# Scale of the first tiles by one-element instructions, and low weights last in the first products

## The chip, the cores and the metric

The kernel runs on one core of one Trainium2 chip. The metric is the device time of one execution in microseconds (us). Five engines work side by side, each with an instruction queue of its own: PE (matrix products; PEld is its loading of weights), DVE (vector), ACT (scalar and activation), POOL (GpSimd) and SP, which here issues all DMAs. They wait for each other through semaphores.

## The reference

```python
x = A_x                                   # 1 x 2048 x 640
xn = _layernorm(x)                        # (x - mean) / sqrt(var + 1e-5)
s = _A_ref(xn, A_wqkv, A_wo)              # attention, 32 heads of 20, window of 8 keys at stride 2, then @ wo
g = _silu(_B_ref(xn, B_w_gate, B_w_up, B_w_down))   # ((xn @ w_gate) * (xn @ w_up)) @ w_down, 1536 wide
return x + s * g
```

Everything is float32.

## The kernel before

**Precision by split.** A matrix in float32 is kept as two matrices: a high part (`hi`, an ACT copy into the rounded type that PE reads, line 85 for weights and 213 for x) and a low part (`lo`, raw minus high, line 86 on POOL for the first weights, line 214 on DVE for x). A product is then three products that add up in one PSUM tile: high by high, then first high by second low, then first low by second high. `mm3` (lines 88 to 93) writes that order out: all K chunks of the first kind, all of the second, all of the third. For `qkv` the first operand is x and the second the weights; for `gate_up_half` the first is the weights and the second x.

**Tiles.** The 2048 positions are 16 tiles of 128 rows. K is 640, that is 5 chunks of 128. `norm(s, n)` normalises n tiles from tile s: `moments` (bn_stats and bn_aggr on DVE), `rstd` (lines 187 to 195), `apply` (line 198, one tensor_scalar of 128x640 per tile with mean and scale as per-row pointers). `trans(s)` (lines 210 to 214) transposes a tile on PE in two groups (4 chunks and 1), into PSUM tiles with tag `q`, of which there are 4; ACT writes the high part, DVE the low part. `rstd` takes a square root on ACT, a sum and a reciprocal on DVE, and corrects the reciprocal by one Newton step: 1.5 - 0.5 * (var + eps) * a * a, times a. It is called for tile 0, tile 1, tiles 2 and 3 together, tiles 4 to 7, and once for the 8 odd tiles.

**Order.** The schedule is manual: each engine executes in the order in which the program issues to it. The head of the program, from its line 616 on, is in turn: `norm(0, 1)`, `moments` of tile 1, the split of the first three chunks of the first attention weights, `trans(0)`, one idle product to keep PE at work, the split of the last two chunks, `norm(1, 1)`, `moments` of tiles 2 and 3, `qkv(0, 0)`, `trans(1)`, the split of the first gate and up weights in five pieces, `norm(2, 2)`, `qkv(0, 1)`, the split of the next gate and up weights, `gate_up_first`, `trans(2)`, `trans(3)`, then `norm(4, 4)` and the following tiles. `split_wq` and `split_wf` put the high parts on ACT and the low parts on POOL. Four idle products run ahead of all this (line 155).

`gate_up_first` (lines 408 to 413) does the first 256 columns, two tiles, of the gate and the up product of the first 128 features, since only two tiles are there by then; `gate_up(0, 0, part=part0)` does the other 256 later and evicts both.

**After the head.** 12 attention units (6 groups of heads by even and odd positions) run on DVE while PE computes the next `qkv` and gate and up pieces; then the output projection, the preparation of the down weights (`sum_wd`, `split_wd`), and the down product by a scheme of 7 products for 8 blocks (`product`), which ends the kernel.

Of the kernel before, what the change touches and what calls it, by code (L numbers as in the profile page):

```python
# [14 lines left out]
ALU = mybir.AluOpType  # L15
# [11 lines left out]
KD, KF = D // P, F // P  # L27
CH = 512
# [11 lines left out]
EPS = 1e-5  # L40
# [10 lines left out]
def kernel(  # L51
# [11 lines left out]
    nc = tc.nc  # L63
# [11 lines left out]
    def st(shape, tag, bufs, dt=F32):  # L75
        cnt[0] += 1
        return sb.tile(shape, dt, tag=tag, bufs=bufs, name=f"{tag}_{cnt[0]}")

    def pt(shape, tag, bufs):
        cnt[0] += 1  # L80
        return ps.tile(shape, F32, tag=tag, bufs=bufs, name=f"{tag}_{cnt[0]}")
# [3 lines left out]
        nc.scalar.activation(hi, raw, AF.Copy)  # L85
        eng.tensor_sub(lo, raw, hi.bitcast(F32))  # L86

    def mm3(acc, pairs, first=True, last=True):

        pairs = list(pairs)  # L90
        runs = [(a[i], b[j]) for i, j in ((0, 0), (0, 1), (1, 0)) for a, b in pairs]
        for n, (a, b) in enumerate(runs):
            nc.tensor.matmul(acc, a, b, start=first and n == 0, stop=last and n == len(runs) - 1)  # L93

# [20 lines left out]
    wf_raw, wf = {}, {}  # L115
# [51 lines left out]
    xT = []  # L167
# [10 lines left out]
    def moments(s0, n, mv=None):  # L178
        stats = st([P, n, 2, 6], "stats", 2)
        mv = st([P, n, 2], "mv", 2) if mv is None else mv  # L180
        for i in range(n):
            for a in range(2):
                nc.vector.bn_stats(stats[:, i, a, :], xt[s0 + i][:, a * HALF:(a + 1) * HALF])
            nc.vector.bn_aggr(mv[:, i, :], stats[:, i])
        return mv

    def rstd(var, out, n):
        r = st([P, 4, NE], "rstd", 2)[:, :, :n]
        nc.scalar.activation(r[:, 0, :], var, AF.Sqrt, bias=eps_t)
        nc.vector.tensor_scalar_add(r[:, 1, :], var, EPS)  # L190
        nc.vector.reciprocal(r[:, 2, :], r[:, 0, :])
        nc.vector.tensor_mul(r[:, 3, :], r[:, 2, :], r[:, 2, :])
        nc.vector.tensor_mul(r[:, 3, :], r[:, 3, :], r[:, 1, :])
        nc.vector.tensor_scalar(r[:, 3, :], r[:, 3, :], -0.5, 1.5, op0=ALU.mult, op1=ALU.add)
        nc.vector.tensor_mul(out, r[:, 3, :], r[:, 2, :])
# [4 lines left out]
    def norm(s0, n, mv=None):  # L200
        mv = moments(s0, n) if mv is None else mv
        r = st([P, n], "r", 2)
        rstd(mv[:, :, 1], r, n)
        for i in range(n):
            apply(xt[s0 + i], mv[:, i, 0:1], r[:, i:i + 1])

    def trans(s):
        hi, lo = xT_tile(s)
        for k0, k1 in ((0, 4), (4, KD)):
            p = pt([P, k1 - k0, P], "q", 4)  # L210
            for k in range(k0, k1):
                nc.tensor.transpose(p[:, k - k0, :], xt[s][:, k * P:(k + 1) * P], ident)
            nc.scalar.activation(hi[:, k0:k1, :], p, AF.Copy)  # L213
            nc.vector.tensor_sub(lo[:, k0:k1, :], p, hi[:, k0:k1, :].bitcast(F32))
# [52 lines left out]
            nc.gpsimd.memset(kv_t[u][0:1, :, 0:W - 1, :], 0.0)  # L267
            kv_zero[r] = GROUPS[g]

    def qkv(u, i):  # L270
        g, r = UN[u]
        c = GROUPS[g] * DH
        p = pt([P, 3 * c], "q", 4)
        hi, lo = xT[(r * NE + i) // TPC]
        t0 = (i % TPC) * P
        a, b = (hi[:, :, t0:t0 + P], lo[:, :, t0:t0 + P]), wq[g]
        mm3(p, [([t[:, k, :] for t in a], [t[:, k, :] for t in b]) for k in range(KD)])
        nc.scalar.activation(kv_t[u][:, :, W - 1 + i, :], p[:, c:].rearrange("p (a c) -> p a c", a=2), AF.Copy)  # L278
        nc.scalar.activation(q_t[u][:, i, :], p[:, :c], AF.Copy)
        for i0, i1 in ((1, 5), (5, NE)):  # L280
            if i == i1 - 1:
                for p0, p1 in ((0, 112), (112, 127)):
                    nc.sync.dma_start(kv_t[u][p0 + 1:p1 + 1, :, i0 - 1:i1 - 1, :],
                                      kv_t[u][p0:p1, :, W - 1 + i0:W - 1 + i1, :])
# [77 lines left out]
    credit = [0]  # L362


    def gate_up_half(f, ch, n, p, c=slice(0, CH)):
        mm3(p[:, c], [([t[:, k, n, :] for t in wf[f]], [t[:, k, c] for t in xT[ch]]) for k in range(KD)])

    def gate_up(f, ch, between=(), amid=(), part=None):
        if part is None:
# [2 lines left out]
        else:  # L372
            pp, c = part, slice(CH // 2, CH)
        gate_up_half(f, ch, 0, pp[0], c)
        for act in amid:
            act()
# [5 lines left out]
        finish_piece()  # L382
        advance(PACE * 3.25 * share)
        gate_up_half(f, ch, 1, pp[1], c)

        def finish():
# [21 lines left out]
    def gate_up_first(f, ch):  # L408

        pp = [pt([P, CH], "g", 2), pt([P, CH], "u", 2)]  # L410
        for n in range(2):
            gate_up_half(f, ch, n, pp[n], slice(0, CH // 2))
        return pp


# [2 lines left out]
    def load_wo(ks):  # L418
        t = st([P, 2, D], "wraw", 3)
        for n, k in enumerate(ks):  # L420
            nc.sync.dma_start(t[:, n, :], wo[:, k, :])
            wo_raw[k] = t[:, n, :]
        return t
# [33 lines left out]
    def out_proj(s):  # L457
        a = oT.pop(s)
        y = st([P, D], "gs", 2)
        for n in range(2):  # L460
            c = slice(n * HALF, (n + 1) * HALF)
            p = pt([P, HALF], "q", 4)
            mm3(p, [([t[:, k, :] for t in a], [t[:, c] for t in wo_s[k]]) for k in range(KD)])
            nc.scalar.activation(y[:, c], p, AF.Copy)
        nc.sync.dma_start(s_scr[s], y)
# [157 lines left out]
    norm(1, 1, mv1)  # L623
    begin_unit(0, False)
    mv2 = moments(2, 2)
    qkv(0, 0)
    trans(1)
    load_x(13, 1, xa[:, 1:2])
    split_wf(0, nc.gpsimd, range(KD + 1))
    norm(2, 2, mv2)  # L630
    qkv(0, 1)
    split_wf(1, nc.gpsimd, range(KD + 1))
    zero_front(0)
    part0 = gate_up_first(0, 0)
    trans(2)
    trans(3)
    mask = st([1, NE, W], "mask", 1)
    nc.gpsimd.memset(mask, 0.0)
    for i in range(NE - 1):
# [3 lines left out]
                          ident.rearrange("p (q i) -> p q i", i=QB).unsqueeze(2).to_broadcast([P, NQ, NQ, QB]))  # L643
    norm(4, 4)
    qkv(0, 2)
    qkv(0, 3)
    gate_up(0, 0, part=part0)
# [13 lines left out]
    load_xq(15, 1, xd)  # L661
    nc.vector.tensor_copy(mro[:, 0, :], mvo[:, :, 0])
    rstd(mvo[:, :, 1], mro[:, 1, :], NE)
    gate_up(0, 1, amid=(spread,))
    trans_odd(8)
# [61 lines left out]
    for ch in range(NCH):  # L727
        gate_up(f0, ch)
        if ch == 0:
# [3 lines left out]
            t = load_wo((4,))  # L733
# [20 lines left out]
    for s in range(NT):  # L754
        k, part = divmod(s - 1, 2)
# [27 lines left out]
    for m in range(n_prod):  # L783
        n, j = divmod(m, 7)
# [59 lines left out]
```

## Time and profile before

| | |
|---|---|
| median of 3 runs | 790.14 us (789.95 to 790.39) |
| the profiled execution | 791.53 us |
| its span | 789.7 us |
| granted PE clock, mean | 0.998 |
| PE busy | 779.9 us, 99% |
| DVE busy | 662.2 us, 84% |
| ACT, POOL busy | 235.0 us, 148.2 us |
| PE busy in 0 to 5, 5 to 10, 10 to 15, 15 to 20, 20 to 25 us | 3.63, 4.47, 4.05, 4.78, 4.54 us |

A row of the timeline gives the start and the duration in us, the engine, the line of the program, the operation, the tiles written and read with their shapes, and a count where equal rows were merged; in brackets stands how long the engine was idle before it and what ended that. The time of a DVE row runs from its issue to its end, so a row that is held by something shows a long duration, not an idle gap. Rows of one engine can overlap at their ends. A list of waits gives the engine and line that waited, the engine and tile it waited for, the sum in us, how often, and the longest.

### The profile page before, as it was taken

The page shows a single profiled execution, that of the slowest core. Times are in us where ns is not written, and L with a number is a line of the kernel's source. Part 1 is how long each engine was busy: PE and PEld are TensorE (multiplying, and loading weights), DVE is VectorE, ACT ScalarE, POOL GpSimd, SP SyncE. Part 2 cuts the span into 40 slices and gives each one's busy share as a digit, 9 for nine tenths or more (in the row PEclk, how much of TensorE's full clock was granted, in tenths as well). Part 3 has the DMA queues.
Part 4 walks back from the last instruction along what each step waited for, and adds up shares of the span by engine and source line. Part 5 has one row for each costly group of instructions (what it writes and reads, how often), then busy time and mean ns, then how long its engine had stood idle before and what let it go on. Part 6 is the DMA issues. An engine that isn't in the chain of part 4 may idle for free. (4 is left out here: it accounts for less than half of the span.)

```text
span 789.7 us, 11220 instructions
## 1 busy us (share of the span) xinstructions
PE 779.9 (99%) x4456; PEld 709.0 (90%) x4456; DVE 662.2 (84%) x657; ACT 235.0 (30%) x536; POOL 148.2 (19%) x110
## 2 busy tenths in 40 slices
PE   8999999999999999999999999999999999999997
PEld 6889898889898898898898989888889999999997
DVE  7889899999999979996999999991268667787775
ACT  4334211121112111311221212112256554444442
POOL 5201211022013200510231000113367600000000
PEclk9999999999999999999999999999999999999999
DMA  8272122141132322404033132322896574555533
GB/s 306 80 229 74 42 59 73 48 123 48 49 84 87 95 71 61 118 27 111 28 104 85 57 85 71 106 88 66 176 249 207 168 279 134 202 207 180 180 101 134
DMA packets 81517, 92.68 MB, mean 117 GB/s; under 512 B 23016, under 2 KB 63032, under 8 KB 81336
## 3 DMA queue, kind: packets, MB, share of 16 engines
q1 hardware_dynamic: 81464, 91.96, 38.1%
q8 instruction: 35, 0.57, 0.3%
q14 instruction: 18, 0.15, 0.1%
HBM read 54.53 MB, written 28.31 MB: 105 GB/s over the span
## 5 line engine op out<-in xcount | busy, mean ns | idle before, releaser
L93 PE MATMUL g<-xc,wf 128*128 128x512 f32 (+1 forms) x735 | 176.2, 390 | 0.1
L93 PE MATMUL u<-xc,wf 128*128 128x512 f32 (+1 forms) x735 | 176.1, 390 | 0.0
L93 PEld LDWEIGHTS u<-xc,wf 128*128 128x128 f32 x735 | 135.6, 187 | 32.2
L93 PEld LDWEIGHTS g<-xc,wf 128*128 128x128 f32 x735 | 135.3, 187 | 31.3 <-POOL wf L86 0.3
L93 PE MATMUL q<-wqh,xc 128*128 128x300 f32 (+1 forms) x960 | 159.9, 309 | 1.3 <-ACT xc L213 0.8
L93 PEld LDWEIGHTS q<-wqh,xc 128*128 128x128 f32 x960 | 146.1, 188 | 3.9 <-ACT xc L213 1.7
L310 DVE TENSOR_TENSOR t<-q,kv 128x1600 f32<-128x1600 f32 (+1 forms) x48 | 98.0, 2042 | 10.1 <-DMA kv<-kv 10.1
L331 DVE TENSOR_TENSOR t<-e,kv 128x1600 f32<-128x1600 f32 (+1 forms) x48 | 97.6, 2051 | 1.1
L86 POOL TENSOR_TENSOR wf<-wraw,wf 128x256 fp32r<-128x256 f32 (+2 forms) x22 | 49.8, 2281 | 247.5 <-ACT wf L85 247.5
L313 DVE TENSOR_REDUCE lg<-t 128x80 f32<-128x1600 f32 (+1 forms) x48 | 92.6, 1930 | 1.2
L378 ACT ACTIVATE gs<-g 128x512 f32<-128x512 f32 x48 | 28.7, 598 | 205.8 <-PE g L93 197.1
L93 PE MATMUL q<-wql,xc 128*128 128x300 f32 (+1 forms) x480 | 86.5, 310 | 0.5 <-POOL wql L86 0.4
L339 DVE TENSOR_TENSOR t<-t,t 128x1600 f32<-128x1600 f32 (+1 forms) x36 | 80.2, 2228 | 1.1
L93 PEld LDWEIGHTS q<-wql,xc 128*128 128x128 f32 x480 | 74.4, 188 | 0.9 <-POOL wql L86 0.9
L278 ACT ACTIVATE kv<-q 128x200 f32<-128x200 f32 (+1 forms) x96 | 33.5, 349 | 131.8 <-PE q L93 131.8
L586 PE MATMUL q<-xc,wf 128*128 128x320 f32 x432 | 67.3, 309 | 0.0
L586 PEld LDWEIGHTS q<-xc,wf 128*128 128x128 f32 x432 | 64.3, 188 | 0.0
L86 POOL TENSOR_TENSOR wql<-wraw,wqh 128x300 fp32r<-128x300 f32 (+4 forms) x15 | 34.0, 2297 | 141.7 <-ACT wqh L85 141.7
L93 PE MATMUL q<-wf,wf 128*128 128x320 f32 x156 | 36.2, 313 | 1.3 <-ACT wf L85 1.3
L93 PEld LDWEIGHTS q<-wf,wf 128*128 128x128 f32 x156 | 25.9, 188 | 2.2 <-ACT wf L85 2.0
L389 DVE TENSOR_TENSOR hs<-u,gs 128x512 f32<-128x512 f32 x39 | 26.6, 683 | 0.4 <-issue 0.4
L86 DVE TENSOR_TENSOR wf<-ot,wf 128x640 fp32r<-128x640 f32 x13 | 14.3, 1098 | 13.8 <-ACT wf L85 12.9
(157 smaller groups left out, 892.5 us busy)
## 6 DMA issues: line engine op xcount, KB each, us to landing
h_scr<-hs SPq DMA_DIRECT2D x48, 256.0 KB, 2.3
wraw<-in_wgu SPq DMA_DIRECT2D x12, 640.0 KB, 5.1
t<-h_scr SPq DMA_DIRECT2D x8, 768.0 KB, 7.6
s_scr<-gs SPq DMA_DIRECT2D x16, 320.0 KB, 3.5
hs<-s_scr SPq DMA_DIRECT2D x16, 320.0 KB, 4.4
gs<-in_x SPq DMA_DIRECT2D x16, 320.0 KB, 4.9
out<-q SPq DMA_DIRECT2D x15, 320.0 KB, 2.4
wraw<-h_scr SPq DMA_DIRECT2D x12, 384.0 KB, 5.6
```

Source lines behind the costliest of these rows:

```text
L86: eng.tensor_sub(lo, raw, hi.bitcast(F32))
L93: nc.tensor.matmul(acc, a, b, start=first and n == 0, stop=last and n == len(runs) - 1)
L278: nc.scalar.activation(kv_t[u][:, :, W - 1 + i, :], p[:, c:].rearrange("p (a c) -> p a c", a=2), AF.Copy)
L310: nc.vector.tensor_mul(t, q.rearrange("p i c -> p (i c)").unsqueeze(1).to_broadcast([P, 2, NE * c]), places(0, j))
L313: nc.vector.tensor_reduce(out=lg[:, :, j:j + 2].rearrange("p n a -> p a n"), in_=heads(t), op=ALU.add, axis=AX.X)
L331: nc.vector.tensor_mul(heads(t), pw, heads(places(1, j)))
L339: nc.vector.tensor_add(acc, acc, t)
L378: nc.scalar.activation(gs, pp[0], AF.Copy)
L389: nc.vector.tensor_mul(hs, pp[1], gs)
L586: nc.tensor.matmul(p, y[:, i, k], wd_t[name][k][:, l], start=new and r == 0, stop=r == len(runs) - 1, skip_group_check=True)
```

## The change

Three edits.

In `rstd`, where one or two tiles are normalised, the instructions work on one element per partition. The sum with eps is one instruction per tile. After the reciprocal, the two multiplications, the Newton factor and the last multiplication (four instructions, three of them tensor_tensor with two tensors as inputs) become three tensor_scalar instructions per tile, with the other factors as per-row pointers: b = a * a * ve, then b = -0.5 * b + 1.5, then out = b * a. For one tile that is 5 DVE instructions in place of 6, for two tiles 9 in place of 6. Calls with four or eight tiles keep the old form.

In the first call of `qkv` the order of the three kinds of products becomes high by high, low part of x by high weights, high part of x by low weights.

In `gate_up_first` the products with low weights of both the gate and the up part come after all others; the partial sums stay open in their two PSUM tiles in between.

The number of products does not change, and on ACT, POOL and SP the instructions and their order are the same.

```diff
-    def mm3(acc, pairs, first=True, last=True):
+    ALL3 = ((0, 0), (0, 1), (1, 0))
+
+    def mm3(acc, pairs, parts=ALL3, first=True, last=True):
 
         pairs = list(pairs)
-        runs = [(a[i], b[j]) for i, j in ((0, 0), (0, 1), (1, 0)) for a, b in pairs]
+        runs = [(a[i], b[j]) for i, j in parts for a, b in pairs]
...
         nc.scalar.activation(r[:, 0, :], var, AF.Sqrt, bias=eps_t)
-        nc.vector.tensor_scalar_add(r[:, 1, :], var, EPS)
+        step = 1 if n <= 2 else n
+        for i in range(0, n, step):
+            nc.vector.tensor_scalar_add(r[:, 1, i:i + step], var[:, i:i + step], EPS)
         nc.vector.reciprocal(r[:, 2, :], r[:, 0, :])
+        if step == 1:
+            for i in range(n):
+                ve, a, b = (r[:, k, i:i + 1] for k in (1, 2, 3))
+                nc.vector.tensor_scalar(b, a, a, ve, op0=ALU.mult, op1=ALU.mult)
+                nc.vector.tensor_scalar(b, b, -0.5, 1.5, op0=ALU.mult, op1=ALU.add)
+                nc.vector.tensor_scalar(out[:, i:i + 1], b, a, None, op0=ALU.mult)
+            return
         nc.vector.tensor_mul(r[:, 3, :], r[:, 2, :], r[:, 2, :])
         nc.vector.tensor_mul(r[:, 3, :], r[:, 3, :], r[:, 1, :])
         nc.vector.tensor_scalar(r[:, 3, :], r[:, 3, :], -0.5, 1.5, op0=ALU.mult, op1=ALU.add)
         nc.vector.tensor_mul(out, r[:, 3, :], r[:, 2, :])
...
-    def qkv(u, i):
+    def qkv(u, i, parts=ALL3):
...
-        mm3(p, [([t[:, k, :] for t in a], [t[:, k, :] for t in b]) for k in range(KD)])
+        mm3(p, [([t[:, k, :] for t in a], [t[:, k, :] for t in b]) for k in range(KD)], parts)
...
-    def gate_up_half(f, ch, n, p, c=slice(0, CH)):
-        mm3(p[:, c], [([t[:, k, n, :] for t in wf[f]], [t[:, k, c] for t in xT[ch]]) for k in range(KD)])
+    def gate_up_half(f, ch, n, p, c=slice(0, CH), **parts):
+        mm3(p[:, c], [([t[:, k, n, :] for t in wf[f]], [t[:, k, c] for t in xT[ch]]) for k in range(KD)], **parts)
...
         pp = [pt([P, CH], "g", 2), pt([P, CH], "u", 2)]
-        for n in range(2):
-            gate_up_half(f, ch, n, pp[n], slice(0, CH // 2))
+        for parts, first in ((ALL3[:2], True), (ALL3[2:], False)):
+            for n in range(2):
+                gate_up_half(f, ch, n, pp[n], slice(0, CH // 2), parts=parts, first=first, last=not first)
         return pp
...
-    qkv(0, 0)
+    qkv(0, 0, ((0, 0), (1, 0), (0, 1)))
```

## The prediction

> **What bounds the kernel now.** I read the page first, then the list of who waited for whom on PE, then the timeline of the first 25 us, because the change touches nothing later.
>
> ```profile
> span 789.7 us, 11220 instructions
> PE 779.9 (99%) x4456; PEld 709.0 (90%) x4456; DVE 662.2 (84%) x657; ACT 235.0 (30%) x536; POOL 148.2 (19%) x110
> ```
>
> PE is the bound. It is idle for 9.8 us of 789.7, and its list of waits says where:
>
> ```profile
> PE q L93 <- ACT wf L85: 1.3, 2, 0.7
> PE q L93 <- ACT xc L213: 0.8, 2, 0.6
> PE q L93 <- DVE xc L214: 0.5, 1, 0.5
> PE q L93 <- POOL wql L86: 0.4, 1, 0.4
> ```
>
> Columns: sum, times, longest, in us. The first line lies at 582.7 and 588.1; the others all lie before 21 us. Asked of 30 to 560 us, the list is empty, so what PE gains in the head arrives at 560 whole, if nothing with a fixed time stands between. The head (start, duration, engine, line, operation):
>
> ```profile
> 8.71 0.14 DVE L190 TENSOR_SCALAR rstd<-mv 128x1 f32<-128x1 f32 x1
> 8.94 0.16 DVE L191 RECIPROCAL rstd<-rstd 128x1 f32<-128x1 f32 x1
> 9.14 0.52 DVE L192 TENSOR_TENSOR rstd<-rstd 128x1 f32<-128x1 f32 x1
> 9.69 0.74 DVE L193 TENSOR_TENSOR rstd<-rstd 128x1 f32<-128x1 f32 x1
> ...
> 10.47 0.19 PEld L93 LDWEIGHTS q<-wql,xc 128*128 128x128 f32 x1 [0.59 <-POOL wql L86]
> 10.48 0.41 PE L93 MATMUL q<-wql,xc 128*128 128x300 f32 x1 [0.37 <-POOL wql L86]
> ...
> 10.86 0.62 DVE L198 TENSOR_SCALAR t<-t,mv,r 128x640 f32<-128x640 f32 x1
> ...
> 11.54 0.53 PEld L212 LDWEIGHTS q<-ident,t 128*128 128x128 f32 x5 [0.21 <-PE q L93]
> ...
> 14.17 0.68 DVE L190 TENSOR_SCALAR rstd<-mv 128x2 f32<-128x2 f32 x1
> ...
> 16.96 0.19 PEld L93 LDWEIGHTS g<-xc,wf 128*128 128x128 f32 x1 [0.32 <-POOL wf L86]
> ```
>
> L86 on POOL, taken alone, has pieces at 8.01, 8.80 and 9.58 (0.84 to 0.85 each) and, from 13.38, ten pieces of 0.74 one every 0.70. Every two-input DVE instruction issued inside a piece ends 0.01 to 0.03 after the piece: 9.66 against 9.65, 10.43 against 10.42. The tensor_scalar of two elements at 14.17 does so as well. So two tiny rows hold up DVE from 9.14 to 10.43, and trans(1) starts when two things are done at nearly the same time: L198 (11.48) and qkv(0,0) on PE (last product started near 11.3).
>
> **norm(0).** Five instructions in place of six: one of about 0.19 (4.98 to 5.17) saved, L198 at 5.37. It is worth nothing: trans(0) also stands behind PE's warm-up products to about 6.1, and its eviction on ACT (7.29) behind the third L85, which waited for a DMA. The cover is ACT's order, not DVE's.
>
> **norm(1).** No row shows a one-element tensor_scalar with a pointer as its scalar. Without a hold its price lies between 0.14 (8.71, immediate scalar) and 0.30 (L198 with two pointers on 160 elements: 1.18 for four); I take the 0.19 from start to start of the small rows, which it resembles most. After the reciprocal (9.14) three of them give 9.14, 9.33, 9.52, and L198 is issued at 9.72. That one has 640 elements and is held like the pair at 17.66 and 18.58, which waited for a piece's end and then took 0.35: piece five ends at 10.42, L198 at about 10.78. Before: 11.48, so 0.70 earlier. At 0.30 a row L198 comes at 9.93 and still ends at 10.78; at 0.14 it comes just before piece five, delays it by 0.25 (POOL's row grew from 0.74 to 0.99 behind such an L198), and PE loses that.
>
> **qkv(0,0) with the low weights last.** Passes of five products take 0.70. First pass as before, from 7.92; the second, low part of x times high weights, at 9.02, since L214 ended at 8.79; the third at 9.72, with pieces one to four ready at 9.65. Its fifth product waits until 10.48 as now, but nothing stands behind it: PE's result is there at 10.89, before 11.58, so 0.69 earlier. trans(1) needs both this and L198, and either part alone would leave it where it is; together it starts 0.69 earlier, at about 10.88. What follows moves with it: L278, L213 (12.24), qkv(0,1) (12.89), the L85 that starts POOL's ten pieces (13.38). DVE's statistics of tiles 2 and 3 start at 10.7; their load, issued at 4.50 with 5.5 to landing, is there at 10.0.
>
> **gate_up_first.** Thirty products of 128x256, one per 0.121 (1.82 for 15 weight loads). Low weights are now asked for after twenty of them: 14.36 + 2.43 = 16.8. POOL's fifth piece of wf ends at 16.91 - 0.69 = 16.2, or 16.7 if both L198 of norm(2) delay it by 0.25. The wait of 0.32 goes, with 0.1 to 0.6 to spare. trans(2) starts at 18.94 - 0.69 - 0.32 = 17.93.
>
> **norm(2).** Nine instructions for six, but five rows held at 0.59 to 0.68 and a free one become nine free ones at about 0.19: L198 is issued near 15.5 in place of 17.66 and both end by 17.3. Alone this is worth at most 0.1 (at 0.69 earlier the first L198 would end at 17.97, just when PE comes), but it keeps the 0.32 from being lost. If the two-element reciprocal, whose row at 14.77 lay at a piece's edge, costs 0.74, L198 is still early. Behind trans(2) the chain L213, L214, qkv(0,2) took 2.01 (18.94 to 20.95) and keeps that; the low-weight pass of later tiles is unchanged.
>
> **Sum and carry.** 0.69 + 0.32 = 1.01 us. The loads of tiles 4 to 7 were issued at 9.25 with 8.8 to landing, 18.1, and DVE now asks at 20.8. SP's queue is not reordered; its next issues wait for hs of POOL (30.90, 39.9), which follow PE. The profiled execution took 791.53 us, 1.8 more than its span of 789.7; less 1.01 that is 790.5 with a span of 788.7. Its offset from the median of the three runs (790.14) is 1.4, so the median comes to 789.1. A measurement of this kernel can tell about 0.2%, 1.58 us, from no change; 1.01 us is 0.13%.
>
> **A rule to weigh.** On trace evidence one-element rows are free of POOL: the reciprocal at 8.94 ended at 9.10, deep in a piece that ran to 9.65, and L190 at 8.71 ended at 8.85 where the piece ended at 8.86, while held rows end after it. The second row is thin, since the edge is so near. [...]
>
> **Rivals.**
> *Every one-element tensor_scalar is held.* norm(1): rows end at 9.66 and 10.43, the third is free, L198 runs 10.66 to 11.28: gain 0.20. norm(2), 0.20 earlier, then has eight held rows: with pieces ending every 0.70 from 13.92, L190 twice to 15.32, six more to 19.52, L198 to 20.56. trans(2) starts at 20.6, not 18.94: slower by about 1.65, 791.8. It turns slower once more than four of the eight are held (four held and four at 0.19 put L198 at 17.7, where it was). [...] Against: the row at 8.71. Chance 0.10.
> *Only the pointer forms are held*, as two-input rows are. norm(1) then has two of three held: 9.66, 9.84, 10.43, L198 to 11.07, gain 0.42; norm(2) has four held and four free, the first L198 ends near 18.4, and trans(2) starts near 18.5. Gain 0.45, 789.7. No row for or against; 0.07.
> *The head's gain is given back.* Some transfer keeps its time, or the stage near 570 absorbs it: 790.1. Against: every issue named above waits for PE's products; 0.05.
> *More than the head.* The two waits on L85 at 582.7 (0.71) and 588.1 (0.54) stand behind DVE rows stretched by POOL (L495 1.15 at 584.20, 0.48 at 573.66). A slightly different meeting of the two could remove both: between 0.6 and 1.25 on top, 788.2. Against: that stage is released by PE and should move as a block; 0.09.
>
> **How the numbers follow.** The forecast, 789.1, has 0.69, with a spread of 0.75 to 1.2 us of gain. The range 788.4 to 790.3 holds it, the pointer rival and the gain given back; it leaves out the held rows (0.10) and most of the last rival (0.08). Faster by over 0.2%: 0.08 from the last rival and 0.02 of the forecast's tail, 0.10. Slower by over 0.2%: 0.06 of the held rows, whose price sits on the bound, and 0.02 for the stage near 582 going the other way, 0.08. The rest, 0.82, is within.
>
> **What would show it.** Right: in the changed profile the three small rows behind the reciprocal of norm(1) take 0.15 to 0.25, L198 ends near 10.8, trans(1) starts near 10.9, no wait of PE for POOL's wf near 17, trans(2) near 17.9, qkv(0,2) near 19.9, and the span is 788.7. Wrong: small rows that end with POOL's pieces; trans(1) past 11.2; PE waiting for L198 ahead of trans(2); or a head that is 1 us ahead at 25 us with an end that is not.

## The result and the profile after

| | before | after |
|---|---|---|
| median of 22 runs | 790.08 us (789.33 to 790.78) | 789.08 us (788.34 to 789.75) |
| the profiled execution | 791.53 us | 789.2 us |
| its span | 789.7 us | 787.3 us |

The ratio of the times is 0.9987, with a 95% interval of 0.9981 to 0.9993. The change gains 1.0 us, less than the 0.2% set as the bound and with an interval that excludes no change. The forecast was 789.1.

Two lines of the page of the changed kernel, and what PE waited for (its list also has 1.4 us for the identity matrix at the start, as before the change, and 0.5 us put down to issue):

```profile
span 787.3 us, 11221 instructions
PE 778.0 (99%) x4456; PEld 708.8 (90%) x4456; DVE 658.7 (84%) x658; ACT 234.6 (30%) x536; POOL 147.8 (19%) x110
```

```profile
PE q L95 <- ACT xc L224: 1.0, 2, 0.6
PE q L95 <- DVE xc L225: 0.8, 1, 0.8
PE q L95 <- ACT wf L85: 0.6, 1, 0.6
```

PE's wait for POOL's `wql` is gone. PE still waits for ACT and DVE behind the transposes, and once for L85 near 590. The timeline of the head (line 194 is the old 190, 199 to 201 are the new rows, 209 is the old 198, 95 the old 93, 223 the old 212):

```profile
8.90 0.14 DVE L194 TENSOR_SCALAR rstd<-mv 128x1 f32<-128x1 f32 x1
9.33 0.27 DVE L199 TENSOR_SCALAR rstd<-rstd 128x1 f32<-128x1 f32 x1
9.64 0.15 DVE L200 TENSOR_SCALAR rstd<-rstd 128x1 f32<-128x1 f32 x1
9.83 0.21 DVE L201 TENSOR_SCALAR r<-rstd 128x1 f32<-128x1 f32 x1
9.90 0.85 PE L95 MATMUL q<-wql,xc 128*128 128x300 f32 x5
10.08 0.61 DVE L209 TENSOR_SCALAR t<-t,mv,r 128x640 f32<-128x640 f32 x1
10.79 0.74 PE L223 MATMUL q<-ident,t 128*128 128x128 f32 x5
...
15.42 2.03 DVE L209 TENSOR_SCALAR t<-t,mv,r 128x640 f32<-128x640 f32 x2
16.63 0.75 PE L95 MATMUL g<-xc,wf 128*128 128x256 f32 x5
...
17.80 1.25 PE L223 MATMUL q<-ident,t 128*128 128x128 f32 x10
19.81 0.97 PE L95 MATMUL q<-wqh,xc 128*128 128x300 f32 x5 [0.76 <-DVE xc L225]
```

The same four starts of PE in the kernel before:

```profile
11.57 0.73 PE L212 MATMUL q<-ident,t 128*128 128x128 f32 x5
...
15.05 2.30 PE L93 MATMUL g<-xc,wf 128*128 128x256 f32 x15
...
18.94 1.55 PE L212 MATMUL q<-ident,t 128*128 128x128 f32 x10
20.95 0.96 PE L93 MATMUL q<-wqh,xc 128*128 128x300 f32 x5 [0.46 <-DVE xc L214]
```

The three new rows take 0.27, 0.15 and 0.21 while POOL works (its pieces run 8.66 to 9.49 and 9.44 to 10.28). trans(1) starts at 10.79, not 11.57; trans(2) at 17.80, not 18.94; qkv(0,2) at 19.81, not 20.95.

The two spans differ by 2.4 us, more than the medians. The same product of PE, just ahead of 568, starts at 567.15 before and 566.01 after: 1.15 us, the 1.14 of the head unchanged over 546 us. The rest arises between 568 and 590, where the profile of before waits twice (1.25 us) and that of after once (0.55). The seven other profiles with the same two buffers there wait once, for 0.45 to 0.55, four of them with only a part of the change; so the second wait is taken as that execution's, and that pair overstates the change.

### The profile page after: what moved, and what is told of

The parts are those of the page before. It is cut to its first block, busy times and chain, and to the rows that moved or that the text cites. A ratio compares the mean times of both kernels' runs of the same rounds, so it can differ in the third digit from the quotient of the medians.

```text
span 787.3 us, 11221 instructions
## 1 busy us (share of the span) xinstructions
PE 778.0 (99%) x4456; PEld 708.8 (90%) x4456; DVE 658.7 (84%) x658; ACT 234.6 (30%) x536; POOL 147.8 (19%) x110
## 5 line engine op out<-in xcount | busy, mean ns | idle before, releaser
L86 POOL TENSOR_TENSOR wf<-wraw,wf 128x256 fp32r<-128x256 f32 (+2 forms) x22 | 47.8, 2197 | 247.6 <-ACT wf L85 229.3
L350 DVE TENSOR_TENSOR t<-t,t 128x1600 f32<-128x1600 f32 (+1 forms) x36 | 78.0, 2166 | 1.1
L86 POOL TENSOR_TENSOR wql<-wraw,wqh 128x300 fp32r<-128x300 f32 (+4 forms) x15 | 34.2, 2300 | 142.6 <-ACT wqh L85 142.6
L86 DVE TENSOR_TENSOR wf<-ot,wf 128x640 fp32r<-128x640 f32 x13 | 13.6, 1045 | 14.1 <-ACT wf L85 14.1
```

Source lines behind the costliest of these rows:

```text
L350: nc.vector.tensor_add(acc, acc, t)
```

## The experiments

Starts on PE in one profiled execution of each kernel, in us. "first" is qkv(0,0).

| kernel | first | trans(1) | gate_up_first | trans(2) | qkv(0,2) | median of the runs, and ratio to before |
|---|---|---|---|---|---|---|
| before | 7.92 | 11.57 | 15.05 | 18.94 | 20.95 | |
| order only | 7.97 | 11.46 | 14.94 | 18.86 | 20.88 | 790.08, 0.9999 (0.9990 to 1.0008) |
| scale only | 7.90 | 11.36 | 14.82 | 18.71 | 20.72 | 790.02, 0.9998 (0.9989 to 1.0007) |
| gate only | 7.71 | 11.42 | 14.90 | 18.61 | 20.66 | 789.99, 0.9995 (0.9987 to 1.0004) |
| order and scale | 7.60 | 10.68 | 14.33 | 18.43 | 20.44 | 789.77, 0.9997 (0.9988 to 1.0006) |
| after | 8.12 | 10.79 | 14.29 | 17.80 | 19.81 | 789.08, 0.9987 (0.9981 to 0.9993) |

The four versions between before and after ran on one chip beside each other (before: 790.14). Their intervals are some 1.4 us wide and separate none of them. The heads do, if stretches and not absolute starts are compared, since the start of qkv(0,0) itself varies from 7.60 to 8.32. Over all fourteen profiles of this document:

- From first to trans(1): 3.65, 3.71 and 3.87 us with neither order nor scale, 3.49 and 3.46 with one of them, 2.67 to 3.12 with both, but for one execution of 3.87 whose weights landed late (below).
- From `gate_up_first` to trans(2): 3.89 to 4.10 in the five profiles without the gate edit, 3.71 with it alone, 3.50 or 3.51 in the six of the whole change (four of them with a third buffer for `gs`), 3.55 and 3.83 in two variants of it (below).
- From trans(2) to qkv(0,2): 2.01 to 2.04 in all.

**Order only.** The scale and `gate_up_first` as before, from the change only:

```diff
-    qkv(0, 0)
+    qkv(0, 0, ((0, 0), (1, 0), (0, 1)))
```

> Only the new order of products in the first qkv; scale and gate as before. Theory (two gates: trans(1) needs both the result of qkv(0,0) on PE and L198 on DVE, which before ended within 0.2 us of each other): qkv(0,0) ends near 10.8 in place of 11.58, but L198 still ends near 11.48, so trans(1) starts at 11.5 and the gain is 0 to 0.1 us; qkv(0,2) starts at 20.9, not 20.95. Rival (PE's own wait for POOL was the gate): trans(1) at 10.9, gain 0.7 us, time 789.4.

PE and DVE near trans(1):

```profile
9.98 0.85 PE L95 MATMUL q<-wql,xc 128*128 128x300 f32 x5
11.46 0.74 PE L224 MATMUL q<-ident,t 128*128 128x128 f32 x5 [0.63 <-PE q L95]
```

```profile
9.42 0.72 DVE L204 TENSOR_TENSOR rstd<-rstd 128x1 f32<-128x1 f32 x1
...
10.75 0.61 DVE L210 TENSOR_SCALAR t<-t,mv,r 128x640 f32<-128x640 f32 x1
```

PE is done with the product at 10.83 and then idles for 0.63; the scaled tile (L210 here) is there only at 11.36. The bracket names PE's own product, but that had long ended, so the wait was for DVE: trans(1) starts 0.10 after the tile, as it does before the change (11.47 and 11.57). As the theory had it; the gate is L198. The 0.1 gained came from POOL's fifth piece, which ended 0.30 earlier in that execution (10.12), so that one two-input row was held and not two.

**Scale only.** The new `rstd`, and the old order of all products.

> Only the one-element scale; order of products as before. Theory of two gates: L198 of tile 1 ends near 10.75, trans(1) still behind the wait for POOL's fifth piece, near 11.55, gain at trans(1) 0 to 0.1; L198 of tiles 2 and 3 done near 17.5, the wait for POOL's wf piece near 17 stays at 0.3; whole time 0 to 0.1 below before. Rival (DVE's chain was the gate): trans(1) near 10.9, gain 0.7, time 789.4.

```profile
9.86 0.86 DVE L209 TENSOR_SCALAR t<-t,mv,r 128x640 f32<-128x640 f32 x1
```

```profile
10.42 0.41 PE L95 MATMUL q<-wql,xc 128*128 128x300 f32 x1 [0.38 <-POOL wql L86]
10.67 0.85 PE L95 MATMUL q<-wqh,xc 128*128 128x300 f32 x5
11.36 0.71 PE L223 MATMUL q<-ident,t 128*128 128x128 f32 x5
```

The tile is ready at 10.72 and PE is late: the wait for POOL's fifth piece in the middle, a pass of 0.85 behind it, and trans(1) at 11.36. So the gate is the other one. The head gains 0.23 at qkv(0,2), somewhat more than the 0 to 0.1 expected: before, the last product of qkv(0,0) started at 11.28 and one takes 0.14, so PE could have begun trans(1) at 11.42, and its gate stood 0.15 ahead of DVE's. Removing DVE's gate alone can gain about that, removing PE's alone nothing.

**Gate only.** `gate_up_first` in two passes, the rest as before:

```diff
-        for n in range(2):
-            gate_up_half(f, ch, n, pp[n], slice(0, CH // 2))
+        for parts, first in ((ALL3[:2], True), (ALL3[2:], False)):
+            for n in range(2):
+                gate_up_half(f, ch, n, pp[n], slice(0, CH // 2), parts=parts, first=first, last=not first)
```

> Only the low weights last in gate_up_first. Theory: no wait of PE for POOL's wf near 17, PE done with it 0.32 earlier, but the first L198 of tiles 2 and 3 ends at 18.66 as before, so trans(2) starts near 18.72 in place of 18.94; gain 0.2 us, time 789.9. Rival (independent parts): 0.32. Both: less than the 0.2% that a measurement tells.

From the start of `gate_up_first` to trans(2) PE takes 3.71 us, before 3.89 and in the changed kernel 3.51. The first L198 of tiles 2 and 3 ended at 18.51, and trans(2) started at 18.61 behind it. So 0.18 of the 0.38 comes without the new scale, as expected.

**Order and scale, without the gate.**

> Order of the first qkv and the one-element scale together, gate as before. Theory of two gates: trans(1) near 10.85, gain there 0.7 to 0.8 although each part alone gives 0.1 at most; the wait for POOL's wf near 16.3 stays at 0.3; qkv(0,2) near 20.2; time 0.7 to 0.8 below before, 789.35. Rival (independent parts): the sum of the times of the two parts alone.

```profile
10.68 0.52 PE L223 MATMUL q<-ident,t 128*128 128x128 f32 x3
```

```profile
16.44 0.39 PE L95 MATMUL g<-xc,wf 128*128 128x256 f32 x1 [0.29 <-POOL wf L86]
```

Together they move trans(1) by 0.9 (0.3 of it an earlier start of qkv(0,0)), where each alone moved it by 0.1 and 0.2: this is the two gates. From first to trans(1) it is 3.08 us against 3.65, 3.49 (order) and 3.46 (scale); here 0.33 of the 3.08 is a wait for the last attention weights, which landed at 8.32. What was gained there was partly lost at `gate_up_first`, 4.10 us: the weights of that product landed late too (12.35), so POOL's pieces stood later against PE than before. The time fell by 0.4, not by the 0.7 to 0.8 expected, with an interval that holds both.

**Tiles 2 and 3 in the old form.** The changed kernel, but

```diff
-        step = 1 if n <= 2 else n
+        step = 1 if n < 2 else n
```

> As the changed kernel, but tiles 2 and 3 together keep the old form of the scale (two elements, two-tensor rows). Theory: five rows held at 0.6 to 0.7, the first L198 ends near 17.9 and trans(2) starts near 17.9 to 18.0, 0 to 0.15 us later than in the changed kernel; trans(3) waits 0.3, qkv(0,2) starts near 19.95; time within 0.15 us of the changed kernel. Rival (the scale of tiles 2 and 3 carries a good part of the gain): 0.3 us or more lost.

```profile
17.07 1.93 DVE L209 TENSOR_SCALAR t<-t,mv,r 128x640 f32<-128x640 f32 x2
```

```profile
18.16 0.74 PE L223 MATMUL q<-ident,t 128*128 128x128 f32 x5 [0.16 <-issue]
```

`gate_up_first` to trans(2) takes 3.83 in place of 3.51: the first scaled tile comes at 18.06 and PE is there at about 17.84 (14.33 + 3.51). The 0.32 that the gate edit takes away comes back as a wait for DVE, twice the upper end of what was expected and by the head the rival's figure. The time, 789.53 with a ratio of 0.9987 (0.9978 to 0.9996) to before, is not told apart from the changed kernel's.

**What is held, by width.** The changed kernel, but the Newton factor works on a scratch tile over 4 elements for tile 0, 3 for tile 1, 2 for tile 2, 3 for tile 3 (`bw`, whose first element is `b`):

```diff
-                nc.vector.tensor_scalar(b, b, -0.5, 1.5, op0=ALU.mult, op1=ALU.add)
+                nc.vector.tensor_scalar(bw, bw, -0.5, 1.5, op0=ALU.mult, op1=ALU.add)
```

> As the changed kernel, but the Newton factor row (-0.5 b + 1.5, immediate scalars) works in place on a scratch tile over 4 elements for tile 0, 3 for tile 1, 2 for tile 2 and 3 for tile 3 (the extra elements are not used). [...] Rival 1 (odd counts escape, as one element does): rows of 3 take 0.16, the row of 2 is held. Rival 2 (what is written in one instruction and not the count decides): all take 0.16. The sum is little changed, under 0.3 us.

DVE, then the pieces of POOL that lie across the rows from 9 us on:

```profile
5.15 0.17 DVE L207 TENSOR_SCALAR wide<-wide 128x4 f32<-128x4 f32 x1
...
9.26 0.27 DVE L206 TENSOR_SCALAR wide<-rstd 128x1 f32<-128x1 f32 x1
9.56 0.39 DVE L207 TENSOR_SCALAR wide<-wide 128x3 f32<-128x3 f32 x1
9.99 0.22 DVE L208 TENSOR_SCALAR r<-wide,rstd 128x1 f32<-128x1 f32 x1
...
14.54 0.27 DVE L206 TENSOR_SCALAR wide<-rstd 128x1 f32<-128x1 f32 x1
14.85 0.29 DVE L207 TENSOR_SCALAR wide<-wide 128x2 f32<-128x2 f32 x1
...
15.60 0.24 DVE L207 TENSOR_SCALAR wide<-wide 128x3 f32<-128x3 f32 x1
```

```profile
9.10 0.84 POOL L86 TENSOR_TENSOR wql<-wraw,wqh 128x300 fp32r<-128x300 f32 x1
...
14.37 0.74 POOL L86 TENSOR_TENSOR wf<-wraw,wf 128x256 fp32r<-128x256 f32 x1
...
15.07 0.74 POOL L86 TENSOR_TENSOR wf<-wraw,wf 128x256 fp32r<-128x256 f32 x1
```

The pieces end at 9.93, 15.11 and 15.81; the rows of 3, 2 and 3 elements end at 9.96, 15.13 and 15.83, each 0.02 to 0.03 behind the piece, and each lasts longer than the 0.17 of the row of 4 in tile 0, which came before POOL's first piece. They are held. They look short beside the 0.68 of the two-element row at 14.17 before the change because each came late in its piece. The one-element row at 9.26 ended at 9.53, inside the piece, and the one at 9.99 at 10.21, inside the piece that ran from 9.89 to 10.72: free, with pointers too. So neither rival holds: the rows of 3 (0.39 and 0.24) were held as the row of 2 (0.29) was, and the one-element rows beside them (0.21 to 0.27) were free. The kernel ran once, in 789.95 us, so its time is no evidence.

**A third buffer for gs.** The changed kernel, with `"gs", 3` in place of `"gs", 2` everywhere. `out_proj` evicts each tile of the output projection into `gs`, and SP stores it from there.

> As the changed kernel, with three buffers in place of two for the tile gs, into which the output projection is evicted. Theory (what differs between executions after 560 us is the wait of ACT's eviction for the store of s two tiles before, since its buffer is the same and the DMA engines are 93% busy there): the row of ACT that waited for s_scr from gs near 577 starts 2 to 3 us earlier, the waits of PE for ACT L85 between 568 and 592 (0.6 in the changed profile, 1.3 before) go, and the time falls by 0.5 to 1 us, 788.3. Rival (the waits come from DVE rows held by POOL there): the eviction is earlier, the waits of PE stay, no change of the time.

ACT's waits between 560 and 600, in the changed kernel and then with three buffers:

```profile
ACT wf L85 <- DVE ot L459: 6.8, 5, 1.8
ACT gs L476 <- PE q L95: 4.3, 5, 1.6
ACT gs L476 <- DMA s_scr<-gs: 3.4, 1, 3.4
```

```profile
ACT gs L476 <- PE q L95: 10.9, 8, 1.7
ACT wf L85 <- DVE ot L459: 4.9, 4, 2.1
```

With two buffers the eviction waited 3.4 us for a store, which held up the splits behind it in ACT's queue; PE waited for one of them near 590. That the one wait led to the other through ACT's queue is argued; that both go with the buffer is shown. With three, no wait for that store is in ACT's list, PE's list for these 40 us is empty, and the time is 788.19 (ratio 0.9967, 0.9955 to 0.9980). A second set of runs gave 788.15 (0.9971, 0.9959 to 0.9982). This beats both kernels.

**The same on the kernel before.**

> The kernel before with three buffers for gs, nothing else. Theory (the gain of the third buffer lies after 560 us and has nothing to do with the head): the same gain as it gave on the changed kernel, 1.0 to 1.4 us, time 788.9, and no wait of PE for ACT L85 between 560 and 600. Rival (the waits near 582 depend on when the head arrives there): a gain under 0.5 us, or waits left.

789.28, ratio 0.9987 (0.9978 to 0.9996), 1.2 us below before, and again no wait of PE between 560 and 600, although its head was the latest of all (qkv(0,2) at 21.60). So the buffer's gain does not depend on the head, and the two gains add: 1.0 + 1.2 against 2.3 measured. The profiles agree: from qkv(0,2) to its last product PE takes 761.17 or 761.18 us in all five with three buffers, and 761.91 to 763.39 in the nine with two.

**The changed kernel again.**

> The changed kernel again, beside the two below on one chip. 1.0 us below before, as measured already (0.9987). Its head: tiles 2 and 3 land at 9.6 to 11.3 and the first gate and up weights at 11.1 to 12.9 in the nine profiles so far, while DVE asks for the first at 10.6 and ACT for the second at 12.1; so qkv(0,2) starts between 19.8 and 20.4.

789.44 against 790.46, ratio 0.9987 (0.9978 to 0.9995): the same gain in another set of runs. But its profiled head is almost that of before, with qkv(0,2) at 20.72, outside the 19.8 to 20.4 expected. ACT and PE of that execution:

```profile
9.37 0.45 ACT L85 ACTIVATE wqh<-wraw 128x300 fp32r<-128x300 f32 x1 [1.09 <-DMA wraw<-in_wqkv]
```

```profile
9.88 1.10 PE L95 MATMUL q<-wqh,xc 128*128 128x300 f32 x6 [1.14 <-ACT wqh L85]
```

The fifth chunk of the attention weights landed at 9.35; in the other profiles it was there at 7.6 to 8.5. That execution took 790.44, one of the slowest of its twelve. One execution's head is therefore good to about half a us. Over the four profiles with the changed head as it stands (19.81, 20.72, and 20.38 and 20.14 with three buffers) the mean is 20.26, over the two with the head of before (20.95, 21.60) it is 21.28: 1.0 us, as the times say, though with a scatter this wide so few profiles agree that well only by luck.

**Loads in smaller pieces.** Three buffers, and tiles 2 and 3 loaded by one DMA each, the first gate and up weights by two:

```diff
-    load_x(2, 2, xe[:, 0:2])
-    load_wf(0)
+    load_x(2, 1, xe[:, 0:1])
+    load_x(3, 1, xe[:, 1:2])
+    load_wf(0, (0, 2, KD))
```

> The changed kernel with three buffers for gs, and with the load of tiles 2 and 3 issued as one DMA for each tile and the load of the first gate and up weights as two (2 and 3 of the 5 chunks). Theory (in the changed head these two loads are what is late next, in about half the executions): statistics of tile 2 start near 10.6 and ACT's split at 12.1 in every execution, qkv(0,2) near 19.8, 0 to 0.4 us below the kernel with three buffers alone. Rival (two more issues on SP, each waiting for a semaphore of an earlier DMA, put the later loads back): no gain or up to 0.3 us lost.

788.25, ratio 0.9980 (0.9969 to 0.9991). Beside the version without the split on one chip:

> The changed kernel with three buffers for gs again, beside the version with split loads on one chip. 2.2 us below before (1.0 of the change and 1.2 of the third buffer, which the kernel before with three buffers showed by itself).

> Three buffers and split loads of tiles 2 and 3 and of the first gate and up weights, on the same chip as the version without the split. Theory (late landings cost the changed head 0 to 0.5 us, 0.2 us in the mean): 0.1 to 0.3 us below it. Rival (what varies is the landing of the attention weights ahead of these, which the split does not touch): the same within 0.1 us.

788.42 (0.9982, 0.9971 to 0.9992) with the split loads, 788.15 without. The heads of the two profiles came early (19.86 and 20.01), but the time shows no gain: neither the theory (0.1 to 0.3 below) nor the second rival (within 0.1) was met by the medians, and the intervals allow both. The runs show something else: 5 of the 23 with split loads took 2.0 us or more above their median (790.4 to 791.9), and of the 22 with three buffers and whole loads only one. The ratios count these runs, the medians hide them. No profile caught such an execution, so its cause stays open; that the split put later loads back, as the first rival has it, is possible and not shown.

## Why the prediction was right

Forecast 789.1, measured 789.08, by the mechanism forecast. That the two agree to 0.02 is luck, as the interval of the gain runs from 0.6 to 1.5 us. The span was forecast at 788.7 and was 787.3, mostly since the profile of before had a second wait near 582 that the changed kernel's did not. The points in turn:

*norm(0)* was worth nothing, as said, but not even the 0.19 within DVE came: the row that scales tile 0 is issued at 5.56 in both kernels, because the pointer rows take what the sixth instruction had cost. ACT's third L85 waited for a DMA until 7.13, and qkv(0,0) started at 8.12, not earlier.

*norm(1)*. The new rows were priced at 0.19 from start to start and take 0.31, 0.19 and 0.25, since a row with two pointers lasts 0.27 and one with one pointer 0.21. L209 was issued 0.75 after the first of them and not 0.58, and ended at 10.69 (10.78 forecast). The cover named, that L209 is held to the piece's end anyway, did not act in this execution: L209 took 0.61, as the same row does at 5.56 before POOL's first piece. It was held in six other profiles with both parts (0.76 to 0.98), and the scale alone shows such a row (0.86, to 0.35 behind the piece's end).

*qkv(0,0)* ended without a wait for POOL's fifth piece, which ended at 10.28, not 10.42. First to trans(1) fell from 3.65 to 2.67, more than the 0.69. About 0.3 of this is the execution: POOL's fifth piece ended 2.16 us after the start of qkv(0,0) and not 2.50, so the old rows would have been released earlier there too. That trans(1) has two gates, of which each part alone opens only one, was shown by the two single parts. The prediction took the 0.69 from PE's end; the gate that decides is DVE's, and as that was put at 0.70 the sum did not suffer. In thirteen of the fourteen profiles trans(1) starts 0.10 after L198 or L209 ends, and only with the scale alone is PE later. In the changed kernel PE could have begun at 10.59 and began at 10.79.

*gate_up_first* gains 0.38 (0.32 forecast), *norm(2)* keeps it: put at 0.1 at most by itself, it is worth 0.32 of the head once the other two are in, as the profile with tiles 2 and 3 in the old form shows; no time shows it. The step that failed there took the first held L198 to be ready just as PE comes; it was 0.2 late. The two-element reciprocal, left open at 0.74, took 0.17 (13.97 to 14.14) while POOL worked.

*The reading of held rows* was too wide: not every two-input DVE instruction inside a piece is held. L214, whose first input is a PSUM tile, ran from 13.42 to 14.06 before the change, inside a piece that ran from 13.38 to 14.13. The rows that were held (the small ones 0.52 to 0.74 us before the change) have all their tensors in SBUF.

*Carry.* From qkv(0,2) to that product near 567 PE takes the same in all profiles but one: 546.17 to 546.21 (546.21 before, 546.20 after). The exception is the kernel with the wide rows, 546.79, for which no cause was found.

*The landings* were the weak step. The load of tiles 2 and 3 was taken from one row to be there at 10.0; over the twelve profiles with that load in one piece it was issued at 4.50 and landed between 9.6 and 11.3, and the weights behind them between 11.1 and 12.9. In the changed kernel DVE asks at 10.6 and ACT at 12.1. So these loads are late next, in some executions: trans(1) to `gate_up_first` took 3.65 and 3.85 us in two profiles, whose gate and up weights landed at 12.35 and 12.86, and 3.46 to 3.51 in the twelve others. A part of the spread over executions lies there; others are the landing of the attention weights and, with two buffers, the stage between 568 and 590.

*Rivals.* Held one-element rows (791.8) and held pointer rows (789.7) are excluded by the changed kernel's own rows (0.14 to 0.27 within POOL's pieces) and by the one-element rows of the width experiment; the gain was not given back. The fourth, that waits near 582 fall away as well, did occur in the pair of profiles, but as a difference between executions and not as an effect of the change: those waits come from two buffers and can be removed by themselves.

## What to carry to other kernels

Where an engine waits for two things that end within some tenths of a microsecond of each other, removing one gains no more than the distance between them: look up the second before judging an edit, and test the parts alone and together. In this kernel small tensor_scalar rows next to POOL's splits were free on a single element, also with pointers (0.14 to 0.27 us), while rows of two or three elements were held to the end of the piece (0.24 to 0.68), so several one-element rows cost less here than fewer wider ones (for tiles 2 and 3, 1.33 us from the first row behind the reciprocal to the last, against 2.67). A single pair of profiles can differ by more than the change does: divide the difference at the places where the engine waits, and believe the times for the sum.

## What the runs showed of the hardware

In the experiment on widths a vector tensor_scalar of 2 or 3 elements on an SBUF tile lasted 0.24 to 0.39 us and ended only 0.02 to 0.03 us after the POOL piece (a tensor_tensor, L86) during which it was issued, while one of a single element took 0.14 to 0.27 in the same place. Each pointer scalar added about 0.06 us to a one-element row (0.15, 0.21, 0.27 with none, one, two). A POOL piece of 256 elements grew from 0.74 to about 1.0 us when a 640-element tensor_scalar had waited for the piece before it. The same load, issued at 4.50 us in twelve profiles, landed between 9.6 and 11.3 us.
